# Token chunks in alternating parts, weight conversion moved, chunk ends reordered in a fused attention and MoE kernel

## The chip, the cores and the metric

The kernel runs on one core of one Trainium2 chip. The metric is the device time of one execution in microseconds (us). Engines are called PE (matrix products), ACT (ScalarE), DVE (VectorE), POOL (GpSimd) and SP (SyncE, which issues the DMAs here).

## The reference

```python
def reference(...):
    attn = softmax(causal(q @ k.T / sqrt(64))) @ v      # 4 batches, 12 heads, 448 x 64
    x = attn.transpose(0, 2, 1, 3).reshape(1792, 768)
    h = x @ w_in                                        # 768 x 2048
    P = a[0] + a[1]*h + a[2]*h**2 + a[3]*h**3
    Q = 1 + abs(b[0])*abs(h) + abs(b[1])*h**2
    return (P / (Q + 1e-6)) @ w_out                     # 2048 x 768
...
```

The weights `w_in` and `w_out` come as 64 bit floats; everything else is 32 bit.

## The kernel before

**Attention.** Two heads of one batch are a pair; there are 24 pairs p. The order of the work is a table of words (`FIRST`, `ORDER`, `TAIL`): per pair, in a software pipeline over several pairs, PE transposes q and k (L257), multiplies them (L289), DVE adds the mask and takes the maximum (L300), ACT takes the exponential (L310), POOL multiplies by the reciprocal sum in seven pieces (L324), PE transposes the result (L343) and multiplies with v (L367). ACT and DVE copy what PE leaves (L272, L353, L355), and split the result into a high and a low part, `xh` and `xl` (L377, L380), since all MoE products are made of three passes of rounded 32 bit numbers.

**Weight conversion.** A chunk of 128 hidden columns f has a `w_in` part (n = 0) and a `w_out` part (n = 1): 32 items in all. An item is loaded as raw 64 bit words (L121, L126; three buffers), turned into 32 bit by bit operations and stored to DRAM (L158). In the attention the bit work is POOL L136 and DVE L146 in one pair, POOL L140 and DVE L152 in the next; in the MoE it is POOL L136, ACT L144, DVE L146 and L152 in one step. POOL L136 writes a buffer `u`, of which there are two, so it waits until the store of the item before last has landed. `NC` items are converted in the attention, spread by `quota`; the rest, one per MoE step from step 2. `items` gives the order of all.

**MoE.** The 1792 tokens are four chunks of 512, 512, 384 and 384. A unit is one token chunk with one f, and `w_units` lists the 64 units; step t works on unit t. PE's `p1(t)` makes h (L205, 18 products), and `p2(t)` multiplies the activation g with `w_out` (L520, L521). Between them lie `act_a`, `dve_a`, `dve_a3`, `act_b`, `dve_b`, `dve_b3` (ACT L442 to L444, L464, L467; DVE L449, L452, L457, L471, L474, L480), then `g_hi` (ACT L486) and `g_lo` (DVE L493). PE's order is p1(t+1), p2(t-1), p1(t+2), p2(t). The PSUM tiles of h are two.

**Splitting weights.** `w_hi` (ACT L180) writes the high half of a weight tile, `w_lo` (L188) the low half: on DVE for n = 0, on POOL for n = 1 and for the first three units. The split is made for both uses of n = 0 in the first two token chunks and at the first use of n = 1; then halves are stored (L191) and loaded later (L167). An item not yet stored when its unit's load is due is split straight from `u`. Where the item that step t converts is the `w_out` of unit t itself, `late` is true and `split_w(t, 1)` stands behind the conversion instead of ahead of it. With the numbers of the kernel before, this is so in no step.

**Chunk ends.** When a token chunk, or a part of it, ends, the accumulators are copied out of PSUM: to `part`, if more f are to come (ACT L528, DVE L539), or to `osb` and to the output (L532 to L546); DVE adds `part` where there is one. The accumulators of the next part take the same PSUM tiles.

All engines run their queues in the order in which the program is written.

Of the kernel before, what the change touches and what calls it, by code (L numbers as in the profile page):

```python
# [8 lines left out]
F32 = mybir.dt.float32  # L9
# [3 lines left out]
ALU = mybir.AluOpType  # L13
# [9 lines left out]

NHEAD = -1
HEAD = """
ld@0 ld@1 ld@2 xd.0
"""

FIRST = """
# [3 lines left out]
TAIL = """  # L33
c.1@2 e.6@1 c.0@2 e.0@1 v.1@2 dh@3 a.1@2 sm@1 v.0@2 a.0@2 r@1 dl@3 n.2@1 n.3@1 xr n.5@1 n.0@1 wh.1.0 p1.0 n.4@1
n.6@1 d@2 n.1@1 wl.1.0 c.1@1 c.0@1 aa.0 da.0 dh@2 dl@2 a.1@1 v.1@1 dz.0 a.0@1 v.0@1 p1.1 wh.2.0 ab.0 wl.2.0 db.0 d@1 dy.0
lw.4.0 gh.0 gl.0 wh.0.1 wl.0.1 aa.1 da.1 p1.2 xl dh@1 dl@1 dz.1 ab.1 wh.1.1 wl.1.1 wh.3.0 lw.2.1 xa.11 p2.0
lw.3.1 aa.2 lw.5.0 db.1 wl.3.0 dy.1 wh.4.0 wl.4.0
"""

# [1 line left out]
def kernel(  # L41
# [20 lines left out]
    KF = DFF // P  # L62
    NP = B * HP
# [2 lines left out]
    LN2 = 0.6931471805599453  # L66
    LSH = 60
    QC = 1.0 + 1e-6
    NC = 11
    NR = 3  # L70
    NL = 3
    NWB = (2, 3)
# [9 lines left out]
    ab = const.tile([P, 6], F32, name="ab")  # L82
# [9 lines left out]
    chunks = [(0, 512), (512, 512), (1024, 384), (1408, 384)]  # L92

    HF = KF // 2
    w_units = [(0, f) for f in range(HF)] + [(1, f) for f in range(KF)] + [(0, f) for f in range(HF, KF)]
    w_units += [(b, f) for b in (2, 3) for f in range(KF)]
    n_use = [sum(g == f for _, g in w_units[:t]) for t, (_, f) in enumerate(w_units)]
    w_raw, w_split = {}, {}
    w32 = {
# [9 lines left out]
        return n_use[t] < 2 - n or (n == 0 and w_units[t][1] < HF)  # L109


    items = sorted(w32, key=lambda i: (i[0] >= HF, i[0] - 4 + 2 * i[1], i[1]))
    c_raw, c_u, c_32, stored = {}, {}, {}, set()

    def conv_load(m):
        if m >= len(items):
            return
        f, n = items[m]
        raw = c_raw[m] = cv.tile([P, DM, 2], U32, tag="raw", bufs=NR, name="raw64")
        if n == 0:  # L120
            nc.sync.dma_start(  # L121
                out=raw.rearrange("p (c f) t -> p c (f t)", c=KD),
                in_=moe_w_in[:, f * P:(f + 1) * P].bitcast(U32).rearrange("(c p) f -> p c f", p=P),
            )
        else:
            nc.sync.dma_start(  # L126
                out=raw.rearrange("p m t -> p (m t)"), in_=moe_w_out[f * P:(f + 1) * P, :].bitcast(U32)
            )
# [70 lines left out]
    def p1(t):  # L199
        lo, n_tok = chunks[w_units[t][0]]  # L200
        ps = ps_h.tile([P, 512], F32, tag="h", name="psH")[:, :n_tok]
        wih, wil = w_split.pop((t, 0))
        for n, (w, x) in enumerate(((wih, xh), (wih, xl), (wil, xh))):
            for c in range(KD):
                nc.tensor.matmul(  # L205
                    ps, w[:, c * P:(c + 1) * P], x[c][:, lo:lo + n_tok],
                    start=(c == 0 and n == 0), stop=(c == KD - 1 and n == 2),
                )
        h_t[t] = ps
# [172 lines left out]
        )  # L382

    def quota(p):
        return int(1 <= p < NP - 1)

    steps = [(m, n) for m in range(NC) for n in (2, 3)]
    done = []
# [40 lines left out]


    NU = len(w_units)
    tmp, g_t, acc, osb, part = {}, {}, {}, {}, {}

    def n_of(t):
        return chunks[w_units[t][0]][1]
# [62 lines left out]
    def p2(t):  # L498
        b, f = w_units[t]
        lo, n_tok = chunks[b]  # L500
        nk = n_tok // P
        begins = t == 0 or w_units[t - 1][0] != b
        ends = t == NU - 1 or w_units[t + 1][0] != b
        half_done = ends and f < KF - 1
        if begins:
            for k in range(nk):
                acc[k] = ps_o.tile([P, 512], F32, tag=f"o{k}", name="psO")
            for k in range(0, nk, 2):
                acc["m", k // 2] = ps_o.tile([P, 512], F32, tag=f"o{4 + k // 2}", name="psM")
        woh, wol = w_split.pop((t, 1))  # L510
        gh, gl = g_t.pop(t)
        passes = [(k, n) for n in range(3) for k in range(nk)]
        if ends:
            passes.sort()
        for k, n in passes:
            g, w = ((gh, woh), (gh, wol), (gl, woh))[n]
            g = g[:, k * P:(k + 1) * P]
            first, last = begins and n == 0, ends and n == 2
            m = acc["m", k // 2][:, (k % 2) * 256:(k % 2 + 1) * 256]
            nc.tensor.matmul(acc[k], g, w[:, :512], start=first, stop=last)  # L520
            nc.tensor.matmul(  # L521
                m, g, w[:, 512:], start=first and k % 2 == 0, stop=last, skip_group_check=True
            )
            if not last:
                continue
            if half_done:
                o = part[b, k] = op.tile([P, DM], F32, tag=f"part{k}", name="part")
                nc.scalar.copy(out=o[:, :512], in_=acc[k])  # L528
            else:
                o = osb[k] = op.tile([P, DM], F32, tag="osb", bufs=4, name="osb")  # L530
                if (b, k) in part:
                    nc.vector.tensor_tensor(out=o[:, :512], in0=acc[k], in1=part[b, k][:, :512], op=ALU.add)  # L532
                else:
                    nc.scalar.copy(out=o[:, :512], in_=acc[k])
            if k % 2 or k == nk - 1:
# [12 lines left out]
    def close_r():
        nonlocal gp, tp, ps_h
# [30 lines left out]
    with tc.manual_schedule():  # L580
# [80 lines left out]
        for t in range(2, NU + 1):  # L661
            now = step.get(t, [])
            if t < NU - 2:
                p1(t + 1)
            g_hi(t - 1)
            g_lo(t - 1)
            if t < NU:
                dve_a(t)
                dve_a3(t)
                for m in now[:1]:  # L670
                    conv_step(m, 2)
                late = (w_units[t][1], 1) in [items[m] for m in now]
# [12 lines left out]
            if t + 1 < NU:
                act_a(t + 1)
            if NU - 2 <= t < NU:
                split_w(t, 1)
            if t < NU:
                dve_b(t)  # L690
                for m in now[:1]:
                    conv_step(m, 3)
                dve_b3(t)
                for m in now[1:]:
                    for n in (2, 3):
                        conv_step(m, n)
# [42 lines left out]
```

## Time and profile before

| what | us |
|---|---|
| timed, median of 3 (lowest, highest) | 626.35 (626.31, 629.35) |
| profiled execution, its own time | 630.65 |
| its span, first to last instruction | 628.9 |
| first MoE product (L205) starts | 151.66 |
| PE busy | 612.5 (97%) |
| DVE busy | 507.2 (81%) |
| ACT busy | 429.8 (68%) |
| POOL busy | 179.2 (29%) |

The profile is of one execution. Busy times of different engines overlap. An instruction's time in the trace includes what it is held up after its start, so two neighbours on one engine are best read from start to start. Rows of the trace stand in a section of their own below.

### The profile page before, as it was taken

What the parts mean: (1) busy time and instruction counts of PE and PEld (TensorE: products, weight loads), DVE (VectorE), ACT (ScalarE), POOL (GpSimd) and SP (SyncE); (2) the same over time, 40 slices, a digit from 0 to 9 for tenths busy, and PEclk for the clock granted to TensorE, in tenths of its full rate; (3) what the DMA queues carried; (4) which work ended last, traced back from release to release, by engine and by line L of the source; (5) the groups of instructions that cost most, each with busy time, mean ns of one, the idle gap of its engine ahead of it and who ended that gap; (6) DMA issues with size and microseconds to landing.
All of it is one profiled execution on the core that took longest, in us unless ns stands there. A gap on an engine that the chain in (4) does not pass through costs nothing.

```text
span 628.9 us, 13040 instructions
## 1 busy us (share of the span) xinstructions
PE 612.5 (97%) x4728; PEld 514.6 (82%) x4728; DVE 507.2 (81%) x1039; ACT 429.8 (68%) x939; POOL 179.2 (29%) x252
## 2 busy tenths in 40 slices
PE   8899999899999999999999999999999999999996
PEld 6666666566788888888888888898999999999996
DVE  3999989786799999999999688668866576876564
ACT  4999989887767776767777565554654555765453
POOL 2888867767454421112434100000000000000000
PEclk9999999999999999999999999999999999999999
DMA  9897889787488889987986978547477756567753
GB/s 196 203 230 178 198 228 212 191 209 231 127 276 293 280 316 323 326 309 261 343 296 219 325 291 293 212 155 275 135 252 249 274 204 244 203 204 248 253 196 125
DMA packets 109328, 150.67 MB, mean 240 GB/s; under 512 B 70992, under 2 KB 83280, under 8 KB 109264
## 3 DMA queue, kind: packets, MB, share of 16 engines
q1 hardware_dynamic: 109264, 149.84, 74.4%
q8 instruction: 37, 0.61, 0.4%
q14 instruction: 27, 0.22, 0.1%
HBM read 112.86 MB, written 36.96 MB: 238 GB/s over the span
## 4 chain that ended last, share of the span: by engine, by line
PE 84%; POOL 5%; ACT 4%; issue 3%; DVE 2%; DMA 1%; SPq 1%; POOLq 0%; ACTq 0%; DVEq 0%
PE psH L205 36%; PE psO L520 24%; PE psM L521 13%; POOL e L324 4%; PE psS L289 4%; PE psD L367 3%; ACT e L310 2%; PE psC L343 2%; PE psA L257 1%; DMA w<-u 1%; PE psI L628 1%; SPq L225 1%; POOL u L136 0%; ACT at L353 0%; DVE psS L300 0%
## 5 line engine op out<-in xcount | busy, mean ns | idle before, releaser
L205 PE MATMUL psH<-xh,whl 128*128 128x512 f32 (+1 forms) x768 | 175.8, 364 | 0.2 <-ACT e L310 0.2
L520 PE MATMUL psO<-whl,gh 128*128 128x512 f32 x448 | 159.6, 392 | 0.4 <-ACT gh L486 0.3
L205 PEld LDWEIGHTS psH<-xh,whl 128*128 128x128 f32 x768 | 136.0, 188 | 15.6 <-ACT e L310 0.3
L521 PE MATMUL psM<-whl,gh 128*128 128x256 f32 x448 | 126.2, 282 | 0.0
L464 ACT ACTIVATE u<-w,lnb 128x512 f32<-128x512 f32 (+1 forms) x64 | 43.0, 671 | 87.4 <-DVE w L449 87.4
L520 PEld LDWEIGHTS psO<-whl,gh 128*128 128x128 f32 x448 | 84.0, 188 | 18.7 <-ACT gh L486 1.5
L205 PE MATMUL psH<-xl,whl 128*128 128x512 f32 (+1 forms) x384 | 87.5, 362 | 0.0
L324 POOL TENSOR_SCALAR e<-e,r 128x192 f32<-128x192 f32 (+6 forms) x168 | 81.6, 510 | 18.1 <-DVE r L320 5.8
L521 PEld LDWEIGHTS psM<-whl,gh 128*128 128x128 f32 x448 | 84.5, 189 | 1.3
L310 ACT ACTIVATE e<-psS,nm 128x448 f32<-128x448 f32 (+6 forms) x168 | 77.4, 485 | 8.3 <-DVE nm L300 7.8
L520 PE MATMUL psO<-whl,gl 128*128 128x512 f32 x224 | 81.0, 390 | 0.0
L205 PEld LDWEIGHTS psH<-xl,whl 128*128 128x128 f32 x384 | 70.1, 188 | 7.6
L442 ACT ACTIVATE u<-psH 128x512 f32<-128x512 f32 (+1 forms) x64 | 34.5, 540 | 53.4 <-PE psH L205 53.3
L300 DVE CUSTOM_DVE_ANT_0 psS<-psS,mask 128x64 f32<-128x64 f32 (+6 forms) x168 | 65.4, 455 | 4.3 <-PE psS L289 4.2
L493 DVE TENSOR_TENSOR gl<-p,gh 128x384 fp32r<-128x384 f32 (+1 forms) x62 | 38.3, 618 | 34.7 <-ACT gh L486 34.7
L136 POOL TENSOR_SCALAR u<-raw 128x768 f32<-128x768 f32 x32 | 39.3, 1228 | 86.3 <-DMA w<-u 58.9
L521 PE MATMUL psM<-whl,gl 128*128 128x256 f32 x224 | 63.2, 282 | 0.0
L188 DVE TENSOR_TENSOR whl<-w,whl 128x768 fp32r<-128x768 f32 x43 | 41.7, 971 | 25.0 <-ACT whl L180 25.0
L471 DVE SCALAR_TENSOR_TENSOR w<-w,u 128x512 f32<-128x512 f32 (+1 forms) x64 | 46.7, 729 | 11.1 <-ACT u L467 11.1
L449 DVE SCALAR_TENSOR_TENSOR w<-w,bb,u 128x512 f32<-128x512 f32 (+1 forms) x64 | 48.7, 760 | 6.7 <-ACT w L443 6.7
L289 PE MATMUL psS<-qkt 64*64 64x256 f32 (+6 forms) x672 | 50.0, 405 | 1.6 <-ACT e L310 1.3
L486 ACT CAST gh<-p 128x512 fp32r<-128x512 f32 (+1 forms) x64 | 36.8, 575 | 20.8 <-DVE p L480 20.7
(64 smaller groups left out, 995.9 us busy)
## 6 DMA issues: line engine op xcount, KB each, us to landing
whl<-whl SPq DMA_DIRECT2D x88, 768.0 KB, 4.2
w<-w SPq DMA_DIRECT2D x56, 384.0 KB, 4.9
raw<-in_moe_w_in_dram SPq DMA_DIRECT2D x16, 768.0 KB, 5.4
raw<-in_moe_w_out_dram SPq DMA_DIRECT2D x16, 768.0 KB, 6.1
w<-u SPq DMA_DIRECT2D x29, 384.0 KB, 3.2
qraw<-in_q_dram SPq DMA_DIRECT2D x48, 112.0 KB, 3.6
kraw<-in_k_dram SPq DMA_DIRECT2D x48, 112.0 KB, 3.5
out_dram<-osb SPq DMA_DIRECT2D x14, 384.0 KB, 2.8
```

Source lines behind the costliest of these rows:

```text
L136: nc.gpsimd.tensor_scalar(out=u.bitcast(F32), in0=y, scalar1=0.0, scalar2=1.0, op0=ALU.mult, op1=ALU.mult)
L188: eng.tensor_tensor(out=w[:, 1], in0=src, in1=w[:, 0].bitcast(F32), op=ALU.subtract)
L205: nc.tensor.matmul(ps, w[:, c * P:(c + 1) * P], x[c][:, lo:lo + n_tok], start=(c == 0 and n == 0), stop=(c == KD - 1 and n == 2),)
L289: nc.tensor.matmul(pss[p, b][half((1 + b + j) % 2)], QK[p][half(j), 0, b * QB:(b + 1) * QB], QK[p][half(j), 1, :b_w[b]], start=True, stop= ...
L300: nc.vector.tensor_tensor_reduce(out=s, in0=s, in1=mask[:, S - w:], scale=-SCALE, scalar=3e38, op0=ALU.add, op1=ALU.min, accum_out=nmx[p][ ...
L310: nc.scalar.activation(out=E[p % 2][i][:, :w], in_=pss[p, i], func=AF.Exp, bias=nmx[p][:, i:i + 1], scale=-1.0, accum_out=SUM[p % 2][:, i, ...
L324: nc.gpsimd.tensor_scalar(out=e, in0=e, scalar1=REC[p][:, i:i + 1], scalar2=0.0, op0=ALU.mult, op1=ALU.add)
L449: nc.vector.scalar_tensor_tensor(out=w, in0=w, scalar=bb[:, 0:1], in1=u, op0=ALU.add, op1=ALU.mult)
L464: nc.scalar.activation(out=r, in_=w, func=AF.Ln, scale=2.0 ** -LSH, bias=lnb[:, 0:1])
L471: nc.vector.scalar_tensor_tensor(out=w, in0=w, scalar=QC, in1=r, op0=ALU.add, op1=ALU.mult)
L520: nc.tensor.matmul(acc[k], g, w[:, :512], start=first, stop=last)
L521: nc.tensor.matmul(m, g, w[:, 512:], start=first and k % 2 == 0, stop=last, skip_group_check=True)
```

## The change

The first 16 units of each of the first two token chunks are taken in other portions: before, chunk 0 with f 0 to 7, chunk 1 with f 0 to 15, chunk 0 with f 8 to 15; now chunk 0 with f 0 to 3, chunk 1 with 0 to 7, chunk 0 with 4 to 11, chunk 1 with 8 to 15, chunk 0 with 12 to 15. The parts begin at steps 0, 4, 12, 20 and 28. Partial results of both chunks are kept, and added to where a third part follows.

`NC` goes from 11 to 6: the attention converts six items, in pairs 5 to 21 but not in those with p % 3 = 1, in 12 POOL and 12 DVE instructions instead of 22 and 22; the first raw loads go to pairs 2, 3 and 5. The MoE converts 26 items in steps 2 to 27, in an order by groups of four f. In this order eleven steps (2, 3, 9 to 11, 17 to 19, 25 to 27) have `late` true.

At a part's end `dve_b` and `dve_b3` of the next unit stand ahead of the copies (`ahead`); the small accumulators of the 384-token chunks get a PSUM tile each; the very last output tile goes out in two DMAs, the wide part first.

```diff
-ld@0 ld@1 ld@2 xd.0
+ld@0 ld@1 ld@2
...
-lw.4.0 gh.0 gl.0 wh.0.1 wl.0.1 aa.1 da.1 p1.2 xl dh@1 dl@1 dz.1 ab.1 wh.1.1 wl.1.1 wh.3.0 lw.2.1 xa.11 p2.0
+lw.4.0 gh.0 gl.0 wh.0.1 wl.0.1 aa.1 da.1 p1.2 xl dh@1 dl@1 dz.1 ab.1 wh.1.1 wl.1.1 wh.3.0 lw.2.1 xa.6 p2.0
...
-    NC = 11
+    NC = 6
...
-    w_units = [(0, f) for f in range(HF)] + [(1, f) for f in range(KF)] + [(0, f) for f in range(HF, KF)]
-    w_units += [(b, f) for b in (2, 3) for f in range(KF)]
+    parts = [(0, 0, 4), (1, 0, 8), (0, 4, 12), (1, 8, 16), (0, 12, 16), (2, 0, 16), (3, 0, 16)]
+    w_units = [(b, f) for b, lo, hi in parts for f in range(lo, hi)]
...
-    items = sorted(w32, key=lambda i: (i[0] >= HF, i[0] - 4 + 2 * i[1], i[1]))
+    items = sorted(w32, key=lambda i: (i[0] // 4, i[0] + 2 * i[1], i[1]))
...
-        return int(1 <= p < NP - 1)
+        return int(5 <= p < NP - 2 and p % 3 != 1)
...
-            if half_done:
-                o = part[b, k] = op.tile([P, DM], F32, tag=f"part{k}", name="part")
+            if not x and half_done and (b, k) in part:
+                o = part[b, k][:, :512]
+                nc.vector.tensor_tensor(out=o, in0=acc[k], in1=o, op=ALU.add)
+            elif not x and half_done:
+                o = part[b, k] = op.tile([P, DM], F32, tag=f"part{b}{k}", name="part")
                 nc.scalar.copy(out=o[:, :512], in_=acc[k])
...
+                if final and k == nk - 1:
+                    nc.sync.dma_start(out=out[r, :512], in_=o[:, :512])
...
-            if p in (1, 2):
-                conv_load(p)
+            if p in (2, 3, 5):
+                conv_load((2, 3, 5).index(p))
...
+            ahead = 1 < t < NU and w_units[t - 1][0] != w_units[t][0]
+            if ahead:
+                dve_b(t)
+                dve_b3(t)
             p2(t - 1)
...
```

First place, ACT, one MoE step in which POOL splits the `w_out` of its unit. In the kernel before, at steps 4 and 5 (`u` is a converted item, `raw` its upper words):

```order
L442 ACTIVATE u<-psH 128x512
L443 ACTIVATE w<-psH,bb 128x512
L444 ACTIVATE p<-psH,na 128x512
L180 CAST whl<-u 128x768
L486 CAST gh<-p 128x512
L180 CAST whl<-u 128x768
L464 ACTIVATE u<-w,lnb 128x512
L467 ACTIVATE u<-u,lnb 128x512
L144 ACTIVATE raw_3672<-raw_3672 128x768
```

And ACT in a step of the changed kernel with `late` true (the first L180 reads what the step's own conversion has just written):

```order
L442 ACTIVATE u<-psH 128x512
L443 ACTIVATE w<-psH,bb 128x512
L444 ACTIVATE p<-psH,na 128x512
L180 CAST whl<-u 128x768
L180 CAST whl<-w 128x768
L486 CAST gh<-p 128x512
L464 ACTIVATE u<-w,lnb 128x512
L467 ACTIVATE u<-u,lnb 128x512
L144 ACTIVATE raw_3043<-raw_3043 128x768
```

Both L180 now stand ahead of L486, the high half of g.

Second place, DVE at the end of the first part of a token chunk, before (copies of `psM` are the small accumulators):

```order
L146 SCALAR_TENSOR_TENSOR u<-raw_3906,u 128x768
L539 COPY part<-psM 128x256 x4
L471 SCALAR_TENSOR_TENSOR w<-w,u 128x512
L474 SCALAR_TENSOR_TENSOR p<-p,na,u 128x512
L152 SCALAR_TENSOR_TENSOR u<-raw_3906,u 128x768
L480 SCALAR_TENSOR_TENSOR p<-w,p 128x512
L188 TENSOR_TENSOR whl<-w,whl 128x768
```

And DVE at the end of the first part in the changed kernel:

```order
L146 SCALAR_TENSOR_TENSOR u<-raw_3043,u 128x768
L471 SCALAR_TENSOR_TENSOR w<-w,u 128x512
L474 SCALAR_TENSOR_TENSOR p<-p,na,u 128x512
L480 SCALAR_TENSOR_TENSOR p<-w,p 128x512
L556 COPY part<-psM 128x256 x4
L152 SCALAR_TENSOR_TENSOR u<-raw_3043,u 128x768
L188 TENSOR_TENSOR whl<-w,whl 128x768
```

L471, L474 and L480, which g waits for, moved ahead of the four copies, and L152 behind them.

## Rows read from the trace of the kernel before

**Rows 1.** The page: the chain that ended last, shares by engine.
```profile
PE 84%; POOL 5%; ACT 4%; issue 3%; DVE 2%; DMA 1%; SPq 1%; POOLq 0%; ACTq 0%; DVEq 0%
```

**Rows 2.** Waits of PE, 0 to 151.7: sum in us, times, longest.
```profile
PE psC L343 <- POOL e L324: 8.0, 13, 1.1
```

**Rows 3.** Waits of POOL, 15 to 165, same columns.
```profile
POOL u L136 <- DMA w<-u: 14.1, 6, 3.0
```

**Rows 4.** Windows by pair: us; PE, PEld, DVE, ACT, POOL busy; clock; DMA share, GB/s.
```profile
47.32:52.91 5.59, 5.59 (x99) 3.99 (x96) 5.59 (x21) 5.57 (x20) 4.80 (x9) 1.00 0.80 155
...
64.24:69.71 5.47, 5.47 (x98) 3.64 (x95) 5.47 (x21) 5.47 (x21) 4.01 (x8) 1.00 1.02 271
...
80.85:88.50 7.65, 6.26 (x98) 4.52 (x96) 5.92 (x22) 6.47 (x23) 5.42 (x9) 1.00 0.72 165
88.50:93.90 5.40, 5.40 (x99) 3.58 (x96) 5.40 (x21) 4.92 (x19) 3.52 (x8) 1.00 0.98 256
...
131.21:138.88 7.67, 6.16 (x98) 4.40 (x96) 5.66 (x22) 6.33 (x23) 5.51 (x9) 1.00 0.72 177
138.88:144.90 6.02, 6.02 (x66) 3.27 (x62) 4.91 (x20) 4.46 (x15) 3.52 (x8) 0.72 1.02 308
```

**Rows 5.** Waits of PE from 150 to the end.
```profile
PE psO L520 <- ACT gh L486: 0.3, 1, 0.3
```

**Rows 6.** PE in time: start, us, instruction; p2 of two neighbouring steps begins.
```profile
310.27 0.39 PE L520 MATMUL psO<-whl,gh 128*128 128x512 f32 x1
...
318.53 0.39 PE L520 MATMUL psO<-whl,gh 128*128 128x512 f32 x1
```

**Rows 7.** A step in time, POOL's L136 beside DVE instructions that read PSUM.
```profile
235.03 0.95 DVE L188 TENSOR_TENSOR whl<-w,whl 128x768 fp32r<-128x768 f32 x1
...
237.39 0.90 POOL L136 TENSOR_SCALAR u<-raw 128x768 f32<-128x768 f32 x1 [8.17 <-DVE w L449]
...
239.42 0.69 DVE L471 SCALAR_TENSOR_TENSOR w<-w,u 128x512 f32<-128x512 f32 x1
...
240.68 0.95 DVE L152 SCALAR_TENSOR_TENSOR u<-raw,u 128x768 uint32<-128x768 uint32 x1
...
242.15 0.95 DVE L188 TENSOR_TENSOR whl<-w,whl 128x768 fp32r<-128x768 f32 x1
```

**Rows 8.** A step in time with POOL's L188 and L136 in it.
```profile
305.09 0.95 DVE L188 TENSOR_TENSOR whl<-w,whl 128x768 fp32r<-128x768 f32 x1
...
308.98 1.60 POOL L136 TENSOR_SCALAR u<-raw 128x768 f32<-128x768 f32 x1
...
309.76 1.36 DVE L471 SCALAR_TENSOR_TENSOR w<-w,u 128x512 f32<-128x512 f32 x1
...
313.18 0.95 DVE L188 TENSOR_TENSOR whl<-w,whl 128x768 fp32r<-128x768 f32 x1
313.29 0.62 ACT L486 CAST gh<-p 128x512 fp32r<-128x512 f32 x1 [0.25 <-DVE p L480]
```

**Rows 9.** DVE, ACT and POOL early in the MoE, in time.
```profile
170.12 1.55 ACT L180 CAST whl<-w 128x768 fp32r<-128x768 f32 x2
...
171.02 2.41 DVE L474 SCALAR_TENSOR_TENSOR p<-p,na,u 128x512 f32<-128x512 f32 x1
171.02 1.86 POOL L188 TENSOR_TENSOR whl<-w,whl 128x768 fp32r<-128x768 f32 x1 [2.87 <-ACT whl L180]
...
172.85 1.34 POOL L136 TENSOR_SCALAR u<-raw 128x768 f32<-128x768 f32 x1
...
173.35 1.65 DVE L188 TENSOR_TENSOR whl<-w,whl 128x768 fp32r<-128x768 f32 x1
```

**Rows 10.** DVE in a step that splits straight from u.
```profile
201.83 1.35 DVE L449 SCALAR_TENSOR_TENSOR w<-w,bb,u 128x512 f32<-128x512 f32 x1
```

**Rows 11.** Ends of parts, in time: DVE's copies, DVE's additions.
```profile
229.96 0.74 DVE L539 COPY part<-psM 128x256 f32<-128x256 f32 x2
...
425.18 0.69 DVE L532 TENSOR_TENSOR osb<-psO,part 128x512 f32<-128x512 f32 x1 [2.78 <-PE psO L520]
```

**Rows 12.** The end of the program, in time.
```profile
624.06 0.59 ACT L534 COPY osb<-psO 128x512 f32<-128x512 f32 x1 [0.45 <-PE psO L520]
```

More of the change, by code (lines that the diff above doesn't have):

```diff
@@ L431 @@
     NU = len(w_units)
-    tmp, g_t, acc, osb, part = {}, {}, {}, {}, {}
+    tmp, g_t, acc, osb, part, fresh = {}, {}, {}, {}, {}, set()
     def n_of(t):
@@ L505, in p2 @@
         if begins:
+            each = nk < 4
             for k in range(nk):
                 acc[k] = ps_o.tile([P, 512], F32, tag=f"o{k}", name="psO")
-            for k in range(0, nk, 2):
-                acc["m", k // 2] = ps_o.tile([P, 512], F32, tag=f"o{4 + k // 2}", name="psM")
+            for k in range(0, nk, 1 if each else 2):
+                m = ps_o.tile([P, 512], F32, tag=f"o{nk + (k if each else k // 2)}", name="psM")
+                acc["m", k] = m[:, :256]
+                if not each:
+                    acc["m", k + 1] = m[:, 256:]
         woh, wol = w_split.pop((t, 1))
         gh, gl = g_t.pop(t)
-        passes = [(k, n) for n in range(3) for k in range(nk)]
+        final = t == NU - 1
+        passes = [(k, n, x) for n in range(3) for k in range(nk) for x in range(2)]
         if ends:
-            passes.sort()
-        for k, n in passes:
+            passes.sort(key=lambda i: (i[0], i[2], i[1]) if final and i[0] == nk - 1 else i)
+        for k, n, x in passes:
             g, w = ((gh, woh), (gh, wol), (gl, woh))[n]
@@ L518, in p2 @@
             first, last = begins and n == 0, ends and n == 2
[L519 to L523, printed above, removed]
+            if x:
+                nc.tensor.matmul(
+                    acc["m", k], g, w[:, 512:], start=first and (k % 2 == 0 or nk < 4), stop=last, skip_group_check=True
+                )
+            else:
+                nc.tensor.matmul(acc[k], g, w[:, :512], start=first, stop=last)
@@ L524, in p2 @@
             if not last:
                 continue
-            if half_done:
-                o = part[b, k] = op.tile([P, DM], F32, tag=f"part{k}", name="part")
+            r = slice(lo + k * P, lo + (k + 1) * P)
+            if not x and half_done and (b, k) in part:
[3 more added lines that the diff above has]
+                o = part[b, k] = op.tile([P, DM], F32, tag=f"part{b}{k}", name="part")
@@ L528, in p2 @@
                 nc.scalar.copy(out=o[:, :512], in_=acc[k])
-            else:
-                o = osb[k] = op.tile([P, DM], F32, tag="osb", bufs=4, name="osb")
+                fresh.add((b, k))
+            elif not x:
                 if (b, k) in part:
-                    nc.vector.tensor_tensor(out=o[:, :512], in0=acc[k], in1=part[b, k][:, :512], op=ALU.add)
+                    o = osb[k] = part[b, k]
+                    nc.vector.tensor_tensor(out=o[:, :512], in0=acc[k], in1=o[:, :512], op=ALU.add)
@@ L533, in p2 @@
                 else:
+                    o = osb[k] = op.tile([P, DM], F32, tag="osb", bufs=3, name="osb")
                     nc.scalar.copy(out=o[:, :512], in_=acc[k])
-            if k % 2 or k == nk - 1:
-                for j in range(k - k % 2, k + 1):
-                    m = acc["m", k // 2][:, (j % 2) * 256:(j % 2 + 1) * 256]
-                    if half_done:
-                        nc.vector.tensor_copy(out=part[b, j][:, 512:], in_=m)
+                if final and k == nk - 1:
+                    nc.sync.dma_start(out=out[r, :512], in_=o[:, :512])
+            elif k % 2 or nk < 4:
+                for j in range(k if nk < 4 else k - 1, k + 1):
+                    m = acc["m", j]
+                    if half_done:
+                        o = part[b, j][:, 512:]
+                        if (b, j) in fresh:
+                            fresh.remove((b, j))
+                            nc.vector.tensor_copy(out=o, in_=m)
+                        else:
+                            nc.vector.tensor_tensor(out=o, in0=m, in1=o, op=ALU.add)
@@ L540, in p2 @@
                         continue
+                    o = osb[j]
                     if (b, j) in part:
-                        nc.vector.tensor_tensor(out=osb[j][:, 512:], in0=m, in1=part[b, j][:, 512:], op=ALU.add)
+                        nc.vector.tensor_tensor(out=o[:, 512:], in0=m, in1=o[:, 512:], op=ALU.add)
                     else:
-                        nc.vector.tensor_copy(out=osb[j][:, 512:], in_=m)
+                        nc.vector.tensor_copy(out=o[:, 512:], in_=m)
                     r = lo + j * P
-                    nc.sync.dma_start(out=out[r:r + P, :], in_=osb[j])
+                    if final and j == nk - 1:
+                        nc.sync.dma_start(out=out[r:r + P, 512:], in_=o[:, 512:])
+                    else:
+                        nc.sync.dma_start(out=out[r:r + P, :], in_=o)
@@ L689 @@
             if t < NU:
-                dve_b(t)
+                if not ahead:
+                    dve_b(t)
                 for m in now[:1]:
                     conv_step(m, 3)
[L693 to L696, printed above, removed]
+                if not ahead:
+                    dve_b3(t)
             if t < NU and late:
```

## The prediction

> **What bounds the kernel now.** I read the page first: PE is busy nearly all the time and holds 84% of the chain that ended last, POOL 5% [rows 1]. So time can only be won where PE waits, and is lost wherever something new makes it wait. Next the waits of PE in the two halves. Up to the first MoE product it waited 8.0 us for POOL's e, in 13 places [rows 2]; in the MoE 0.3 us in all [rows 5]. So the attention has something to give, the MoE nothing but something to lose.
>
> The windows by pair say where the attention loses. A pair takes 5.40 us when only PE counts, 5.47 to 5.59 in the middle, where DVE and ACT are busy all the time too, and in the last nine windows, from 80.85 to 138.88, 5.4 and 6.5 to 7.7 in turn [rows 4]. The long ones have POOL behind them: six times L136 waited for a DMA, 14.1 us together [rows 3]. This is the store of the item before last, which must land before `u` is written again; POOL's seven L324 stand in its queue behind L136, and PE's L343 waits for them. The window from 138.88 shows a granted clock of 0.72, a stretch at 1.2 instead of 2.4 GHz, behind the last of these waits [rows 4].
>
> The MoE is read from DVE, the engine nearest to PE. p2 begins every 8.26 us [rows 6]. DVE, from one L188 to the next, takes 242.15 - 235.03 = 7.12 us with a conversion in the step [rows 7], and 313.18 - 305.09 = 8.09 us where POOL's L188 and L136 fall into it [rows 8]. Both are below 8.26, so PE never waits, by 0.17 us in the second kind.
>
> **Attention, part by part.** Six items instead of eleven take away 10 POOL and 10 DVE instructions. More than that, the waits go: items 0 to 2 don't write their result into `u`, and of items 3, 4 and 5 only item 5 reuses a buffer with a store behind it, that of item 3, five pairs old. Without the waits POOL has 3.5 to 4.8 us of work in a pair [rows 4], less than PE's 5.40. What is late next is ACT and DVE, which set 5.47 to 5.59.
> - The nine windows from 80.85 to 138.88 are 58.03 us. At 5.47 each they are 49.2: 8.8 less (7.7 at 5.59, 9.4 at 5.40).
> - The six from 47.32 to 80.85 are 33.5 us; a third of the pairs lose their conversion, at 5.47 it is 32.8: 0.7 less (0 to 1.1).
> - The slow clock: 0.72 over 6.02 us is 1.7 us of PE's work lost; without long waits I expect full clock, 1.7 less (0 to 1.7, as ACT and DVE may be next).
> - Pairs 1 to 4 lose their conversion but ran at PE's pace; the raw load taken out of the head is not waited for there, and the first is needed only in pair 5. Nothing.
>
> Together 11.2 us less (7.7 to 12.2).
>
> **MoE: the late steps.** In eleven steps ACT's split of the unit's own `w_out` now waits for DVE's L152 of the same step. Behind it in ACT's queue stand the other L180 and g's high half, and DVE's L188 waits for the second L180. Counted from the start of L152: L152 0.95, two L180 1.55 together [rows 9], so DVE's L188 is ready at 2.5; it would have started at 242.15 - 240.68 = 1.47 [rows 7]. That is 1.1 us of idle DVE. POOL's L188 starts after the first L180, at 0.95 + 0.78, and lasts 1.86 [rows 9], to 3.6. Now the rows on two engines at once: DVE's L474 started together with POOL's L188 and took 2.41 us, and DVE's L188 beside POOL's L136 1.65 instead of 0.95 [rows 9]; beside L136, L471 took 1.36 instead of 0.69 [rows 7, 8]. In each case DVE's own time starts when POOL has ended. L452 and L457, which read PSUM, are not held up [rows 7]. So in a late step DVE's L188 is held until 3.6, another 1.1 us; and if POOL's L136 of the next item takes its turn right after, as it did ahead of L471, which then took its 1.36 us [rows 8], L493 waits 0.9 more [rows 7]. A late step costs DVE 7.12 + 1.1 + 1.1 = 9.3 us, or 10.2 with L136's turn.
>
> The Trainium skill, page "SBUF — State Buffer", section "Who interferes with whom", says the same as a rule: a DVE instruction with two SBUF inputs and a GpSimd instruction that reads SBUF take one shared pair of ports in turn, the loser blocked until the other has ended. The 2.41 us row agrees. By the rule each turn of L136 would count as soon as it meets such an instruction, which gives the upper end below, 638 us; if the engines only slowed each other a little, the sum would be that of the first rival.
>
> The nine steps 5 to 7, 13 to 15 and 21 to 23 split n = 0 straight from `u`, and L136 waits for DVE's L188 there; where that occurred, L449 took 1.35 instead of 0.74 [rows 10], so 7.1 or 7.7 us. Steps 8, 16 and 24 are of the 8.1 kind. Steps 4, 12 and 20 begin a part: 7.1, and the copies, 4 x 0.37 = 1.5 at steps 4 and 12, and at 20 the additions, 4 x 0.69 + 4 x 0.37 = 4.2, the small ones taken like the copies [rows 11].
>
> DVE's work in steps 2 to 27, against 26 x 8.26 = 214.8 us of PE:
> - every turn taken: 11 x 10.2 + 9 x 7.7 + 3 x 8.1 + 3 x 7.1 + 7.2 = 234.3 us, 19.5 too many;
> - DVE only waits for ACT: 11 x 8.2 + 9 x 7.1 + 52.8 (the rest as above) = 206.9 us, none too many.
>
> What is too many PE waits out, except for DVE's lead. The lead can grow to 4.6 us (p2 at 318.53 less g's high half at 313.29 + 0.62) [rows 6, 8], but what DVE gains in a short step is already in the sum of all steps. Behind step 27 there is no conversion, and nothing is carried on. In the lower case a short queue at the beginnings of parts remains, where ACT's copies stand ahead of the next L442, some 2 us. So the MoE costs 2 to 19.5 us. I take POOL's L188 with its full block, since POOL reaches the ports 0.7 us before DVE, and half of the turns of L136, since it may also wait for its raw load or store and then fall beside the instructions that read PSUM [rows 7]: 11 x 9.75 + 9 x 7.4 + 52.8 = 226.7 us, 11.9 too many. The wait of before, 0.3, goes with the reordering: 11.6 us more.
>
> SP: in a late step the store of the halves (L191) waits for POOL, and with it the store of the item and the next raw load; all three are needed more than a step later. Nothing.
>
> **The end.** The last output tile goes out in two DMAs. The wide copy, 0.59 us [rows 12], can start three small products earlier; 0.2 us less (0 to 0.4).
>
> **Sum.** 630.65 - 11.2 + 11.6 - 0.2 = 630.8 us. The profiled execution is 4.3 us over the median of the runs. As PE waits in the MoE for only 0.3 us, the excess can hardly lie there; it lies in the attention's waits, which the change removes, so I take nothing off, and keep it for the lower end. Against the median the forecast is 0.7% slower.
>
> **The rivals.**
> 1. The late steps are cheap: DVE and POOL hardly meet, as in the 7.12 us steps, and DVE's lead covers the rest. Then 630.65 - 11.2 + 2 - 0.2 = 621.3 us, clearly faster. For it: the kernel before shows both kinds of step, and PE waited in neither. Against it: POOL's split starts in the one stretch of the step in which DVE has only instructions with two SBUF inputs. It decides at a late step of about 8.6 us: then DVE's total reaches that of PE.
> 2. In between: late steps of 9.0 to 9.3 us and few turns of L136, 4 to 9 us of waits, so 623 to 628 us, no difference that can be told.
> 3. The attention doesn't get faster, because ACT and DVE are the bound at 5.59 and the slow clock stays: 7.7 instead of 11.2, and with the forecast's MoE 634.3 us. Against it the 5.40 windows.
>
> **How the numbers follow.** Forecast 0.41 (its own range 628 to 637), rival 1 0.30, rival 2 0.24, rival 3 0.05. About 0.5%, 3.1 us, is what a measurement of this kernel can tell from no change. Above 629.5: most of the forecast's case and rival 3, 0.41; 623.2 to 629.5: rival 2 and the low edge of the forecast, 0.27; below: 0.32. The range of 8 in 10 goes from 619.0 (rival 1 with PE's pace in the attention and part of the 4.3 us) to 636.5 (every turn taken).
>
> **What would show it.** In the profile after: windows by pair of 5.4 to 5.6 from pair 5 on, and no wait of L136 in the attention; the first L205 near 140.5; waits of PE's L520 for g's halves in the MoE, growing over steps 9 to 12, 17 to 21 and 25 to 28; DVE's L188 in late steps stretched to about 2 us beside POOL's L188. If PE's waits in the MoE stay under 3 us, the step on the ports is wrong; if the first L205 isn't before 144, the one on the attention is.

## The result and the profile after

The changed kernel takes 636.41 us (median of four, 634.43 to 637.71); the kernel before, run beside it, 627.75 us. The ratio is 1.0135, 95% interval 1.0092 to 1.0177: slower by 1.3%. The profiled execution took 637.71 us, span 635.9, against 630.65 and 628.9 before.

The span grew by 7.0 us, in four pieces: the first L205, which opens the MoE, starts at 140.64 instead of 151.66, 11.0 us earlier; the steps 2 to 27 (from p2 of step 2 at 174.94 to that of step 28 at 408.83) take 233.9 instead of 215.2 us, 18.7 more; the steps behind them take 0.6 less, and the end 0.1 less.

**The attention.** Windows by pair of the changed kernel (columns as in [rows 4]), and all its waits of POOL from 15 to 160:

```profile
63.90:69.36 5.46, 5.46 (x97) 3.64 (x99) 4.84 (x20) 5.46 (x20) 4.11 (x8) 1.00 0.89 231
...
85.80:91.25 5.45, 5.45 (x97) 3.48 (x98) 5.45 (x21) 5.45 (x20) 4.76 (x8) 1.00 0.83 175
91.25:96.71 5.46, 5.46 (x95) 3.54 (x96) 5.46 (x21) 5.46 (x20) 3.24 (x8) 1.00 0.75 167
```

```profile
POOL e L324 <- PE psS L289: 13.6, 9, 3.8
POOL e L324 <- ACT at L353: 11.9, 5, 2.4
POOL e L324 <- DVE r L320: 11.6, 9, 2.1
POOL whl L188 <- ACT whl L180: 6.4, 3, 2.9
POOL gl L493 <- ACT gh L486: 2.7, 1, 2.7
```

The long windows of [rows 4] are gone, and so is the wait of [rows 3]. A window is left 0.06 us over PE's 5.40. ACT is busy all the time in each of the three, so it is most likely what sets them; this was not tried.

**The MoE.** One late step of the changed kernel in time, DVE, ACT and POOL (start, us, instruction, idle time ahead of it and what ended it):

```profile
241.33 0.95 DVE L152 SCALAR_TENSOR_TENSOR u<-raw,u 128x768 uint32<-128x768 uint32 x1
242.20 0.69 DVE L480 SCALAR_TENSOR_TENSOR p<-w,p 128x512 f32<-128x512 f32 x1
242.32 0.84 ACT L180 CAST whl<-u 128x768 fp32r<-128x768 f32 x1 [0.31 <-DVE u L152]
243.06 0.83 ACT L180 CAST whl<-w 128x768 fp32r<-128x768 f32 x1
243.24 1.84 POOL L188 TENSOR_TENSOR whl<-u,whl 128x768 fp32r<-128x768 f32 x1 [6.55 <-ACT whl L180]
243.80 0.61 ACT L486 CAST gh<-p 128x512 fp32r<-128x512 f32 x1
243.93 1.97 DVE L188 TENSOR_TENSOR whl<-w,whl 128x768 fp32r<-128x768 f32 x1 [1.04 <-ACT whl L180]
245.04 1.59 POOL L136 TENSOR_SCALAR u<-raw 128x768 f32<-128x768 f32 x1
...
245.82 1.37 DVE L493 TENSOR_TENSOR gl<-p,gh 128x512 fp32r<-128x512 f32 x1
247.11 0.74 DVE L449 SCALAR_TENSOR_TENSOR w<-w,bb,u 128x512 f32<-128x512 f32 x1
...
251.28 0.96 DVE L152 SCALAR_TENSOR_TENSOR u<-raw,u 128x768 uint32<-128x768 uint32 x1
```

From L152 to L152 it is 9.95 us, where PE needs 8.26; the eleven late steps take 9.9 to 10.0 us, but for the last (below). Three things in it are longer than in [rows 7]: DVE waits 1.04 us for the second L180; DVE's L188 then takes 1.97 instead of 0.95 and ends 0.8 us behind POOL's L188; and DVE's L493 takes 1.37 instead of 0.69 beside POOL's L136, which began as soon as POOL was free.

PE's waits from 150 to 440, to be read against the one row of [rows 5], and PE in time at the beginnings of p2 of steps 10 and 11 (9.95 apart, against 8.26 in [rows 6]):

```profile
PE psO L529 <- DVE gl L493: 5.2, 4, 1.5
PE psO L529 <- ACT gh L486: 3.8, 7, 0.8
PE psH L205 <- DVE p L457: 1.1, 3, 0.4
```

```profile
244.46 0.51 PE L529 MATMUL psO<-whl,gh 128*128 128x512 f32 x1 [0.25 <-ACT gh L486]
...
254.41 0.50 PE L529 MATMUL psO<-whl,gh 128*128 128x512 f32 x1 [0.76 <-ACT gh L486]
```

The share of PE in the chain that ended last fell from 84% [rows 1] to this, from the page of the changed kernel:

```profile
PE 55%; DVE 23%; issue 12%; ACT 7%; POOL 2%; DMA 1%; POOLq 0%; DVEq 0%; ACTq 0%
```

### The profile page after: what moved, and what is told of

Same layout as the page of the kernel before. It is cut to its first block, busy times and chain, and to the rows that moved or that the text cites. A ratio compares the mean times of both kernels' runs of the same rounds, so it can differ in the third digit from the quotient of the medians.

```text
span 635.9 us, 13038 instructions
## 1 busy us (share of the span) xinstructions
PE 615.8 (97%) x4728; PEld 510.6 (80%) x4728; DVE 526.3 (83%) x1055; ACT 430.1 (68%) x944; POOL 169.5 (27%) x247
## 4 chain that ended last, share of the span: by engine, by line
PE 55%; DVE 23%; issue 12%; ACT 7%; POOL 2%; DMA 1%; POOLq 0%; DVEq 0%; ACTq 0%
PE psH L205 18%; PE psO L529 13%; PE psM L525 7%; PE psS L289 6%; PE psD L367 6%; DVE whl L188 4%; PE psC L343 4%; DVE u L146 3%; DVE w L449 3%; ACT whl L180 3%; DVE p L474 3%; DVE gl L493 3%; ACT e L310 2%; DVE p L452 2%; DVE u L152 2%
## 5 line engine op out<-in xcount | busy, mean ns | idle before, releaser
L205 PE MATMUL psH<-xh,whl 128*128 128x512 f32 (+1 forms) x768 | 176.2, 364 | 1.3 <-DVE p L457 1.1
L529 PE MATMUL psO<-whl,gh 128*128 128x512 f32 x448 | 162.8, 398 | 4.3 <-ACT gh L486 3.8
L205 PEld LDWEIGHTS psH<-xh,whl 128*128 128x128 f32 x768 | 136.0, 188 | 17.6 <-DVE p L457 2.1
L324 POOL TENSOR_SCALAR e<-e,r 128x192 f32<-128x192 f32 (+6 forms) x168 | 77.0, 478 | 47.0 <-DVE r L320 21.6
L529 PE MATMUL psO<-whl,gl 128*128 128x512 f32 x224 | 82.8, 397 | 5.2 <-DVE gl L493 5.2
L205 PE MATMUL psH<-xl,whl 128*128 128x512 f32 (+1 forms) x384 | 87.4, 362 | 0.0
L205 PEld LDWEIGHTS psH<-xl,whl 128*128 128x128 f32 x384 | 70.1, 188 | 7.5
L493 DVE TENSOR_TENSOR gl<-p,gh 128x384 fp32r<-128x384 f32 (+1 forms) x62 | 45.1, 728 | 34.9 <-ACT gh L486 34.9
L136 POOL TENSOR_SCALAR u<-raw 128x768 f32<-128x768 f32 x32 | 42.1, 1316 | 86.3 <-DVE whl L188 71.1
L188 DVE TENSOR_TENSOR whl<-w,whl 128x768 fp32r<-128x768 f32 x33 | 43.4, 1316 | 25.0 <-ACT whl L180 24.6
L449 DVE SCALAR_TENSOR_TENSOR w<-w,bb,u 128x512 f32<-128x512 f32 (+1 forms) x64 | 51.5, 805 | 6.7 <-ACT w L443 6.7
L529 PEld LDWEIGHTS psO<-whl,gl 128*128 128x128 f32 x224 | 42.5, 190 | 15.3 <-DVE gl L493 6.5
L471 DVE SCALAR_TENSOR_TENSOR w<-w,u 128x512 f32<-128x512 f32 (+1 forms) x64 | 42.3, 661 | 10.4 <-ACT u L467 10.4
L289 PE MATMUL psS<-qkt 64*64 64x192 f32 (+6 forms) x672 | 49.0, 398 | 1.9 <-ACT e L310 1.8
```

Of the source, the lines that this page charges most:

```text
L188: eng.tensor_tensor(out=w[:, 1], in0=src, in1=w[:, 0].bitcast(F32), op=ALU.subtract)
L205: nc.tensor.matmul(ps, w[:, c * P:(c + 1) * P], x[c][:, lo:lo + n_tok], start=(c == 0 and n == 0), stop=(c == KD - 1 and n == 2),)
L289: nc.tensor.matmul(pss[p, b][half((1 + b + j) % 2)], QK[p][half(j), 0, b * QB:(b + 1) * QB], QK[p][half(j), 1, :b_w[b]], start=True, stop= ...
L324: nc.gpsimd.tensor_scalar(out=e, in0=e, scalar1=REC[p][:, i:i + 1], scalar2=0.0, op0=ALU.mult, op1=ALU.add)
L449: nc.vector.scalar_tensor_tensor(out=w, in0=w, scalar=bb[:, 0:1], in1=u, op0=ALU.add, op1=ALU.mult)
L471: nc.vector.scalar_tensor_tensor(out=w, in0=w, scalar=QC, in1=r, op0=ALU.add, op1=ALU.mult)
```

## The experiments

Line numbers in a row are those of the kernel that it comes from; where an edit adds lines, L493 becomes L496 or L497, and in e8 L136 becomes L139 and L188 L191. "Steps 2 to 27" is the time from p2 of step 2 to p2 of step 28 less PE's 26 x 8.26 = 214.8 us. "Late step" is DVE's time for one, from an instruction of it to the same instruction a step later; where it goes by one number the steps differ by less than 0.1 us, and step 27, which has no next item to convert, is left out of these.

| kernel | first L205 | steps 2 to 27, over 214.8 | late step | median, us | ratio to before |
|---|---|---|---|---|---|
| before | 151.66 | 0.4 | none | 627.75 | 1 |
| changed | 140.64 | 19.1 | 9.95 | 636.41 | 1.0135 (1.0092 to 1.0177) |
| e1_late_dve | 140.53 | 5.0 | 8.4 to 9.1 | 622.42 | 0.9894 (0.9844 to 0.9943) |
| e2_l136_first | 138.22 | 14.6 | 9.2 to 10.3 | 632.89 | 1.0076 (1.0047 to 1.0106) |
| e3_split_order | 140.03 | 11.4 | 9.4 | 628.69 | 1.0004 (0.9977 to 1.0030) |
| e8_narrow_l136 | 139.80 | 11.5 | 9.3 to 9.4 | 628.82 | 1.0005 (0.9981 to 1.0029) |
| e7_dve_order | 138.25 | 1.3 | 8.0 to 8.7 | 617.71 | 0.9833 (0.9797 to 0.9869) |
| e4_nc8 | 141.21 | 1.9 | none | 619.57 | 0.9848 (0.9787 to 0.9908) |
| e6_nc8_no_ahead | 141.39 | 2.1 | none | 622.16 | 0.9916 (0.9889 to 0.9943) |
| e5_before_u3 | 148.36 | 0.4 | none | 625.58 | 0.9968 (0.9943 to 0.9994) |

The theory: a late step is long because DVE waits for ACT, and then takes turns with POOL, once for POOL's L188 and once for L136. The rivals: POOL's load does not matter, only the place of instructions in the queues; or the loss is in the ends of parts.

**e1_late_dve**: the late split's low half on DVE instead of POOL.

```diff
-        eng = nc.gpsimd if t < 3 or n == 1 else nc.vector
+        eng = nc.gpsimd if (t < 3 and n == 0) or (n == 1 and not is_late(t)) else nc.vector
...
```

> The changed kernel, but in the eleven late steps the low half of the unit's own w_out (L188) is made by DVE, not by POOL. Theory (ports: what a late step costs is mostly DVE waiting for its turn beside POOL's L188 and L136): POOL has only L136 left there, DVE gets 0.87 us more work, and does it while it would wait for ACT; a late step takes 0.95 + 0.83 + 0.87 + 0.87 + 0.6 + 4.2 = 8.3 to 8.5 us instead of 9.95, PE waits in steps 2 to 28 fall from 19 to 2 to 4 us, time 618 to 624 us. Rival (the queue: the cost is that ACT's second L180 and g's high half stand behind a wait for L152): ACT's order is the same and DVE has more to do, so steps stay at 9.9 or get longer, 636 us or more.

Measured 622.42 us, as the theory had it. DVE in a late step:

```profile
248.35 0.94 DVE L188 TENSOR_TENSOR whl<-u,whl 128x768 fp32r<-128x768 f32 x1
...
249.22 0.95 DVE L188 TENSOR_TENSOR whl<-w,whl 128x768 fp32r<-128x768 f32 x1
250.09 0.68 DVE L497 TENSOR_TENSOR gl<-p,gh 128x512 fp32r<-128x512 f32 x1
```

DVE makes both low halves, 1.9 us together, in the time that one of them took beside POOL (1.97), and L497 is then free of L136's turn. L136 takes a turn elsewhere in six of the eleven late steps; these are the ones of 8.7 us and more. The instruction added to DVE, the engine that sets the late steps, made the kernel 14 us faster.

**e2_l136_first**: in a late step the next L136 stands ahead of POOL's L188.

```diff
+                for m in step.get(t + 1, []):
+                    conv_step(m, 1)
...
-            for m in step.get(t + 1, []):
-                conv_step(m, 1)
+            if not (t < NU and late):
+                for m in step.get(t + 1, []):
+                    conv_step(m, 1)
```

> The changed kernel, but in the late steps POOL's L136 of the next item stands ahead of POOL's L188, so that it can run earlier, beside DVE instructions that read PSUM. Theory (ports, every turn counts): L493 is no longer held by L136, a late step takes 9.0 to 9.2 us instead of 9.95, waits of PE fall by 7 to 10 us, time 626 to 630 us. Rival (the queue behind L152 on ACT): nothing that ACT does moves, so 635 to 638 us.

Measured 632.89 us, between the two. POOL and DVE in a late step (step 11, 9.44 us):

```profile
247.50 1.61 POOL L136 TENSOR_SCALAR u<-raw 128x768 f32<-128x768 f32 x1 [5.60 <-DMA w<-u]
248.28 1.38 DVE L480 SCALAR_TENSOR_TENSOR p<-w,p 128x512 f32<-128x512 f32 x1
...
252.07 0.68 DVE L493 TENSOR_TENSOR gl<-p,gh 128x512 fp32r<-128x512 f32 x1
```

L493 is free (0.68), but L136 now waits for a store and falls beside L480, which takes 1.38 instead of 0.69: the turn was moved, not saved. The late steps differ, 9.2 to 10.3 us with a mean of 9.6 (9.9 in the changed kernel): where L136 comes late, POOL's L188 starts behind it, and L493 takes 2.3 us beside that (steps 19 and 26). PE's list of waits now has one for POOL:

```profile
PE psO L529 <- POOL whl L188: 2.7, 3, 1.5
```

The expectation overlooked both. The gain holds one stretch at half clock less in the MoE (below).

**e3_split_order**: the split for three units on, on ACT and DVE, stands ahead of the late split.

```diff
-            if t < NU and late:
-                split_w(t, 1)
             if t + 3 < NU:
                 split_w(t + 3, 0)
+            if t < NU and late:
+                split_w(t, 1)
```

> The changed kernel, but in the late steps the split for unit t + 3 (ACT L180, DVE L188) stands ahead of the late split, so that DVE's L188 doesn't wait for L152's way through ACT. Theory (ports): DVE's L188 runs at once, then POOL's L188 has the ports for 1.8 us and L493 waits for it, L136 takes a turn behind that: a late step takes 9.6 to 9.9 us instead of 9.95, time 632 to 637 us. Rival (the queue): the idle time of DVE goes and with it the cost; late steps of 8.1 to 8.4 us, time 618 to 623 us.

Measured 628.69 us; both missed, since the theory had taken the turns to stay as they were and the rival had taken them to go. DVE's wait for ACT and the block of L188 go, and two others come, L493 beside POOL's L188 and L449 beside L136:

```profile
249.84 0.95 DVE L188 TENSOR_TENSOR whl<-w,whl 128x768 fp32r<-128x768 f32 x1
...
250.60 1.87 POOL L188 TENSOR_TENSOR whl<-u,whl 128x768 fp32r<-128x768 f32 x1 [6.21 <-ACT whl L180]
251.06 1.95 DVE L493 TENSOR_TENSOR gl<-p,gh 128x512 fp32r<-128x512 f32 x1 [0.27 <-ACT gh L486]
252.44 1.31 POOL L136 TENSOR_SCALAR u<-raw 128x768 f32<-128x768 f32 x1
252.94 1.35 DVE L449 SCALAR_TENSOR_TENSOR w<-w,bb,u 128x512 f32<-128x512 f32 x1
```

A late step is 0.6 us shorter, 9.35 here: the wait for ACT fell from 1.04 to 0.27, and the two turns cost together what they had cost before (1.26 and 0.61 us, against 1.02 and 0.68).

**e8_narrow_l136**: only L136's turn is taken away.

```diff
-                out=u.bitcast(F32), in0=y, scalar1=0.0, scalar2=1.0, op0=ALU.mult, op1=ALU.mult
+                out=u[:, x].bitcast(F32), in0=y[:, x], scalar1=0.0, scalar2=1.0, op0=ALU.mult, op1=ALU.mult
...
```

Here `x` is 64 columns behind a late step and all 768 elsewhere, so the kernel leaves out the sign bits of the other columns.

> The changed kernel, with L136 of the item behind each late step cut from 768 to 64 columns (the sign bits of the other columns are left over from an earlier item, so the converted weights are not the reference's); POOL's L188 and every other instruction stay. Theory (L136's turn is the half of the sum that was mis-sized): its turn in front of L493 costs 0.7 to 0.9 us in each of eleven late steps, so late steps go from 9.95 to 9.1 to 9.3 and the time from 636.4 to 626 to 629, and fewer stretches at half clock follow. Rival (L136 takes its turns beside instructions that would wait anyway): late steps stay above 9.7 and the time above 633.

Measured 628.82 us, inside the theory's range; the late step, 9.35, just above its 9.1 to 9.3. L188 keeps its wait and its block, and the instruction behind it, the L493 of the changed kernel, is free. L139 itself waits for DVE's L191 to end, and is done 0.1 us later:

```profile
241.13 2.04 DVE L191 TENSOR_TENSOR whl<-w,whl 128x768 fp32r<-128x768 f32 x1 [1.04 <-ACT whl L183]
242.32 0.95 POOL L139 TENSOR_SCALAR u<-raw 128x64 f32<-128x64 f32 x1
...
243.09 0.72 DVE L496 TENSOR_TENSOR gl<-p,gh 128x512 fp32r<-128x512 f32 x1
```

So L136's turn is worth 19.1 - 11.5 = 7.6 us, what changes of the clock by it (below) included.

**e7_dve_order**: the edits of e1 and e3 together.

> The late split on DVE, and the split for three units on ahead of it: the edits of e1_late_dve and e3_split_order together. Theory (a late step's excess is POOL's turn plus the wait for ACT, and nothing else): DVE has 7.12 + 0.95 = 8.1 us of work in a late step and waits for nothing, so the steps are 8.26 us, PE waits in the MoE only at the ends of parts, and the time is 617 to 620. Rival (the rest of e1's excess is DVE's own work and other turns of POOL, not the wait for ACT): late steps stay at 8.6 to 8.8 and the time at 621 to 624.

Measured 617.71 us, the time of the theory. It beats the kernel before by 1.7% and the changed kernel by 2.9% (617.71 / 636.41), and is the fastest measured here. The late steps, though, are not the 8.1 us that the theory had: they are 8.0 in five and 8.6 to 8.7 in six, where L136 still takes a turn, here ahead of DVE's L188:

```profile
242.91 1.74 POOL L136 TENSOR_SCALAR u<-raw 128x768 f32<-128x768 f32 x1 [7.55 <-DMA w<-u]
...
243.82 1.65 DVE L188 TENSOR_TENSOR whl<-w,whl 128x768 fp32r<-128x768 f32 x1
245.39 0.94 DVE L188 TENSOR_TENSOR whl<-u,whl 128x768 fp32r<-128x768 f32 x1
```

At 0.4 us over PE's 8.26, two such steps in a row are covered by DVE's lead; this is all that PE waits for g in the whole MoE:

```profile
PE psO L533 <- DVE gl L497: 0.2, 1, 0.2
```

That agrees with the point that rival 1 of the prediction named, late steps of about 8.6 us.

**e4_nc8**: eight items in the attention. With eight no step is late; the other lines make room for a third buffer `u`.

```diff
...
-    NC = 6
+    NC = 8
...
-            u = c_u[m] = cv.tile([P, DM], U32, tag="u", bufs=2, name="u")
+            u = c_u[m] = cv.tile([P, DM], U32, tag="u", bufs=3, name="u")
...
-        return int(5 <= p < NP - 2 and p % 3 != 1)
+        return int(5 <= p < NP - 2 and p != 13)
...
-                    o = osb[k] = op.tile([P, DM], F32, tag="osb", bufs=3, name="osb")
+                    o = osb[k] = op.tile([P, DM], F32, tag=f"part{b - 2}{k}", name="osb")
```

> The changed kernel with eight items converted in the attention (pairs 5 to 21 but 13), so that no MoE step is late; three buffers u instead of two, and the output tiles of the last two token chunks in the buffers of the partial results, to make room. Theory: the alternating parts cost nothing by themselves; the attention ends 0.5 to 1.5 us later than in the changed kernel (first L205 at 141 to 142), PE waits 1 to 4 us in the MoE, time 617 to 624 us. Rival (the additions and copies at five ends of parts and the heavier DMA traffic of the alternating order are what costs): steps 12 and 20 stay as long as in the changed kernel, 628 us or more.

Measured 619.57 us, as expected. All of the changed kernel's parts, reordered ends and conversions but two are still in it, and the MoE loses 1.9 us: the loss came from the late steps, not from the five parts.

**e6_nc8_no_ahead**: e4 without DVE's early products at the ends of parts.

```diff
-            ahead = 1 < t < NU and w_units[t - 1][0] != w_units[t][0]
+            ahead = False
```

> The kernel of e4 (eight items in the attention, no late step), with DVE's two products of the next unit behind the chunk end again instead of ahead of it. Theory (the reordered ends are worth what the copies and additions at a chunk end take of DVE): steps at the ends of parts get 1 to 2 us longer at step 20 and 0 to 1 at steps 4, 12, 28; 620 to 623 in all. Rival (DVE's lead covers it, since no late step eats it): no step changes, 619 to 620.

Measured 622.16 us, in the theory's range, but the steps show little of it. Step 19 to 20 takes 9.04 instead of 8.26 us, and the next 8.37 instead of 9.29: the additions are paid for one step earlier, not saved. Up to the last p2 the trace is 1.1 us longer than e4's, 0.2 of them in the attention, which the edit does not touch, and 0.5 at step 32 (7.80 instead of 7.34). The reordered ends are worth about 1 us; the medians' 2.6 us has overlapping intervals.

**e5_before_u3**: the kernel before with three buffers `u`.

```diff
-            u = c_u[m] = cv.tile([P, DM], U32, tag="u", bufs=2, name="u")
+            u = c_u[m] = cv.tile([P, DM], U32, tag="u", bufs=3, name="u")
```

> The kernel before with three u buffers instead of two, nothing else. Theory (what the attention gained in the changed kernel was the wait of L136 for the store of the item before last): the waits of u L136 for a DMA, 14.1 us together before, shrink to under 4 us, the first L205 comes at 140 to 143 instead of 151.66, the MoE keeps 8.26 us a step, and the time is 616 to 620, ratio 0.98 to 0.99. Rival (the number of conversions and their DMA traffic is what held the attention): the first L205 stays above 148, time 624 to 628.

Measured 625.58 us, first L205 at 148.36: the rival's figures. The wait of L136 is gone from the list, but PE's waits from 60 to 150 now begin with another:

```profile
PE psD L367 <- DMA vraw<-in_v_dram: 3.5, 3, 2.5
```

The loads of v stand in SP's queue with the conversion's loads and stores, and land after 9.5 us at the worst instead of 7.5. Its attention also ran longer at half clock than that of the kernel before: a granted clock of 0.80 from 10 to 20 us and 0.86 from 20 to 30, 3.4 us of work lost, against 1.7 there, late in the attention [rows 4]. At equal loss the first L205 would have come some 5 us earlier instead of 3.3 (an estimate from these numbers), still not 11. So the wait for the store was not the whole of it: with eleven items the next wait comes right behind it. With eight (e4) or six it does not. Which of the DMAs delays v, and what the raw load in the head adds, was not tried.

## Why the prediction was right in its sign and short in its size

1. **Attention: right.** Forecast 11.2 us less and a first L205 near 140.5; measured 11.0 and 140.64. Windows of 5.4 to 5.6 and no wait of L136 were the named signs, and both are there. Two smaller things cancel in the sum. The raw load taken out of the head was costed at nothing, but the first pairs came earlier (the second group of L343 starts at 23.48 before, at 20.70 in e7); this edit was not tried alone. And the stretch at half clock was not saved but moved to the first pairs (below): the two kernels without it, e2 and e7, have their first L205 at 138.2. And the reason was too narrow: fewer items, not the two buffers alone, bring the gain (e5).

2. **MoE: the mechanism right, one term mis-sized.** Each term of a late step stands in the trace: 1.04 us for ACT (1.1 in the sum, though its own rows give 2.5 - 1.47 = 1.0), 1.02 for POOL's L188 (1.1), 0.68 for L136's turn (0.9). The step that failed is "half of the turns of L136, since it may also wait for its raw load or store". It did not wait: in all ten late steps that have a next item, L136 took its turn before L493. POOL's L136 stands directly behind POOL's L188, and the row at 245.04 above has no idle time ahead of it, so its raw load and the store that it needs had landed by then. The eleventh late step, 27, has no next item; its L493 is free, and it takes 9.23 us:

```profile
397.01 1.95 DVE L188 TENSOR_TENSOR whl<-w,whl 128x768 fp32r<-128x768 f32 x1 [1.03 <-ACT whl L180]
398.88 0.68 DVE L493 TENSOR_TENSOR gl<-p,gh 128x512 fp32r<-128x512 f32 x1
```

The steps that split straight from `u` took their turns too: DVE's L449 is 1.36 or 1.37 in all nine, as in [rows 10], and DVE needs 7.7 us there. DVE's time for steps 2 to 27 is read from its L452 of steps 2 and 28:

```profile
167.07 0.68 DVE L452 TENSOR_TENSOR p<-p,psH 128x512 f32<-128x512 f32 x1
...
400.15 0.68 DVE L452 TENSOR_TENSOR p<-p,psH 128x512 f32<-128x512 f32 x1
```

It is 233.1 us, where the prediction had 234.3 for "every turn taken" and went on with 226.7. Of the 6.4 us between, the late steps have 1.4 (108.6 against 11 x 9.75), the nine split steps 3.1 (69.7 against 9 x 7.4), and the other 2.0 lie where the prediction had taken no discount: steps 8, 16 and 24 took 8.5 instead of 8.1, and the three beginnings of parts 0.8 more in all.

The rule that the prediction cites, from the Trainium skill, page "SBUF — State Buffer", section "Who interferes with whom", was given its own result there, 638 us; the profiled execution took 637.71. That both agree so well is partly chance: the late steps took 9.9 instead of 10.2, and the steps just named and the half clock (below), which the sum did not have, made up for it.

3. **What was left out of the MoE.** Of the 19.1 us over PE's pace, the trace shows PE idle for 10.6 (233.89 less 223.25 busy). 3.4 are two stretches at half clock, which the prediction did not have. The rest, about 5 us, lies at the waits too. Neighbouring records of products overlap, since one begins 0.12 or 0.23 us after the other and lasts 0.28 or 0.39; a wait breaks this overlap off, and the first record behind it is 0.51 instead of 0.39. The ends of these records are modelled, so it is best counted with the waits. e8, without half clock in its MoE, shows it as well: 11.5 us over PE's pace, 6.9 of them idle.

4. **The end and the parts: right, near nothing.** 0.1 us less at the end (0.2 forecast), 0.6 less in the steps behind 28, where [rows 5] had its 0.3.

5. **The rivals.** Rival 1 and 2 fell with the late step of 9.95. Rival 3 fell with the windows. By time, the median of 636.41 is 0.1 us below the upper end of the range, 636.5, so that it lies inside is luck. The prediction calls that end "every turn taken", but its own terms give 630.65 - 11.2 + 19.5 - 0.3 - 0.2 = 638.45 for it; and the point of 630.8, worked out for the profiled execution, was 6.9 us short of that execution's 637.71, nearly all of it in the MoE.

## What to carry to other kernels

Where a trace shows instructions of two engines taking turns, look at what stands behind such an instruction in the other engine's queue: here it had nothing to wait for, took the next turn in all ten steps, and no discount was due. A step that is a little over the bounding engine's pace is covered by the lead and costs nothing; one that is 1.7 us over it, three in a row, costs nearly all of that. And moving work away from the loaded engine can cost more than leaving it there: 0.95 us of split on DVE was cheaper than 1.84 us on POOL that blocked DVE.

## What the runs showed that was not expected

**Turns alternate.** In a late step of the changed kernel DVE's L188, POOL's L136 and DVE's L493 follow POOL's L188 one after the other, each ending 0.5 to 0.9 us behind the one of the other engine. An L136 of 0.90 us by itself [rows 7] is 1.59 long there, from 245.04 on, and L493 0.69 and 1.37.

**Half clock in the middle of the MoE.** Windows of the changed kernel around its last late steps (columns as in [rows 4]; the clock is the third number from the end):

```profile
323.50:327.90 4.40, 2.13 (x9) 1.01 (x7) 3.37 (x4) 1.57 (x3) 3.36 (x2) 1.00 1.05 407
327.90:331.40 3.50, 3.50 (x11) 3.02 (x12) 3.46 (x6) 2.80 (x5) 0.00 (x0) 0.52 1.01 415
331.40:335.00 3.60, 3.60 (x20) 3.08 (x19) 3.56 (x7) 2.44 (x4) 0.00 (x0) 1.00 1.05 368
395.00:399.50 4.50, 3.04 (x12) 1.74 (x11) 3.47 (x5) 2.18 (x4) 1.82 (x1) 1.00 0.67 258
399.50:403.00 3.50, 3.38 (x11) 2.90 (x12) 3.24 (x6) 2.65 (x5) 0.00 (x0) 0.51 1.01 414
```

Ahead of each stretch PE had waited for part of several steps, 4.40 - 2.13 = 2.3 us of one window; then it ran at 1.2 instead of 2.4 GHz for 3.5 us, 1.7 us of work lost each time. DVE goes on meanwhile, so part of that comes back: the step from 20 to 21 is 8.26 us long here and 9.58 in e8, which has no such stretch. In the MoE e2 shows one such stretch and the other kernels none. A third stretch stands early in the attention of the changed kernel and not in that of e7, though PE was busy for much the same share ahead of it (2.75 and 2.58 of 4 us). First the changed kernel, 12 to 16 and 18.3 to 23.5 us:

```profile
12.00:16.00 4.00, 2.75 (x32) 1.22 (x32) 3.04 (x16) 3.93 (x17) 2.57 (x6) 1.00 0.67 149
18.30:23.50 5.20, 5.20 (x55) 2.86 (x55) 3.07 (x16) 3.86 (x13) 3.21 (x7) 0.77 0.51 137
```

and e7:

```profile
12.00:16.00 4.00, 2.58 (x44) 1.45 (x44) 2.97 (x16) 3.93 (x16) 3.21 (x7) 1.00 0.68 153
18.30:23.50 5.20, 5.20 (x96) 3.56 (x92) 4.28 (x18) 5.14 (x19) 3.00 (x7) 1.00 0.55 139
```

Executions of these two kernels differ by it: those of e7 with a mean clock of 1.0 took 616.7 to 617.1 us, those with 0.997 618.3 to 619.0; those of the changed kernel with 0.991, 0.994 and 0.997 took 637.71, 636.3 to 636.5 and 634.43. It is not all of the spread: executions of the kernel before with a mean clock of 0.995 took 623.7 to 631.0 us. What decides whether a short wait of PE brings the half clock stays open.
